# Written orders for five engines in place of a planner: a scan followed by a mixture of adapters

## The chip, the cores and the metric

The kernel runs on one core of one Trainium2 chip. The metric is the device time of one execution in microseconds (us); lower is better.

## The reference

Two stages follow each other. The first is a linear recurrence along 6400 steps, for 8 sequences of 128 channels. The second takes the 51,200 resulting rows as tokens: a gate picks 2 of 8 adapters, and each token gets its own value plus the weighted output of the two rank-16 adapters.

```python
for t in range(S):                       # S = 6400, a and b are (8, 6400, 128)
    h = a[:, t] * h + b[:, t]
    out[:, t] = h
x = out.reshape(51200, 128)
logits = x @ w_gate                      # 8 experts
topk = the two largest logits of a row
w = softmax over these two
for e in range(8):
    z = x[mask] @ A[e]                   # A[e] is (128, 16), mask: rows that chose e
    delta[mask] += w[mask, k, None] * (z @ B[e])
return x + delta
```

## The kernel before

The 51,200 rows are cut into 100 units of 512 rows. A unit passes through these operations; the letter is the name in the code, with the unit's number behind it.

- The loads ld a, ld b bring rows of `a` and `b` from HBM, two units (512 KB) at a time, into rings of 8 slots each (16 units). SP issues them, and the stores too, in one list.
- AB (line 86, the helper's `transpose`) turns 512 rows of `a` and of `b` on TensorE (PE) into `pA` and `pB`, so that time runs along the free axis. `pA` has one buffer, `pB` two.
- aev (line 491) copies `pA` to `a_st` on ScalarE (ACT).
- scan (line 510) runs the recurrence on VectorE (DVE) and writes `xT` in float16. `xT` is a ring of 16 units (XR): scan w has to wait for the readers of unit w - 16.
- L (line 82) multiplies a unit by the gate's weights into half of a PSUM bank, `pTL`. The units form gate groups of up to 4; for each group, lev (line 583) copies the logits on ACT, and some ten small steps on DVE and GpSimd (POOL), p1 to p7, m1, m2, mx, find the two largest and their difference. sig (line 684) makes the weights `g` on ACT.
- Z (line 82) multiplies the unit by all eight A at once into `pZ` (two buffers). mul (line 729) multiplies by the gate weights, in float16, into `zw`: on DVE, or for 21 units on POOL, after a copy zev (line 715) by ACT.
- T (line 86) transposes `zw` into the other half of the bank `pTL`, and tev (line 786) copies it to `zwT` on ACT. As L and T share that bank, PE and ACT take turns on it.
- R (line 82) puts x itself into `pO` (two buffers) and D (line 82) adds `zwT` times B to it. oev (line 821) copies `pO` to `outt`, a ring of 24 output slots (NOUT), and a store of one or two units takes it to HBM. The store of unit u is held until scan u + 22 is done (HOLD).

The order in which each engine meets these operations is set by a planner, `_Plan.schedule`, before the program is built. Every operation has a due number (its unit plus the offset of its kind in `KEY`) and costs in nanoseconds. The planner walks through time and gives each engine, among the operations that can start soonest, the one with the lowest due number. For a few operations it also chooses the engine. The order is then fixed: each engine runs its list from the front, and an operation whose inputs are not there holds up all behind it. `_Plan.run` writes the waits on semaphores.

The constants are an identity matrix built on POOL (`ident_f`, needed by every transposition) and the weights of the gate, A and B, which ACT's queue loads and POOL casts to float16 (cstg, cstA, cstB). At the start PE runs seven matmuls on an empty tile (`heat`), while the first loads are under way.

Of the kernel before, what the change touches and what calls it, by code (L numbers as in the profile page):

```python
# [12 lines left out]
KEY = {  # L13
    "AB": -228.9, "aev": 79.1, "scan": 140.1, "L": -12.2, "lev": -63.6, "gate": 83.5, "sig": 69.7, "Z": 27.8,
    "mul": -75.3, "zev": 6.2, "T": -117.7, "tev": 38.1, "R": 189.8, "D": 29.2, "oev": 168.4,
}
SLACK = {"pe": 20.0, "dve": 20.0, "act": 0.0, "pool": 60.0, "sp": 120.0}
# [3 lines left out]
POOL_MULS = (2, 10, 4, 2)  # L21
HOLD = 22
FREE = 100
HEATS = 7
WIDE = 100
SOLO = (2, 4)
FUSE = (100, 100)
WIDE8 = 460.0
RING = 8
XR = 16  # L30
NOUT = 24
TAIL = 10
FILLS = 0


class _Op:


    def __init__(self, name, engs, kind, unit, cost, emit, deps, dma, bank, mode):
        self.name = name  # L40
        self.engs = engs
        self.eng = engs[0]
        self.kind = kind
        self.unit = unit
        self.cost = cost
        self.emit = emit
        self.deps = deps
        self.dma = dma
        self.bank = bank
        self.mode = mode  # L50
        self.signal = False
        self.done = None
# [7 lines left out]


# [30 lines left out]
class _Plan:  # L92


    def __init__(self, sems, offset, slack):
        self.sems = sems
        self.offset = offset
        self.slack = slack
        self.ops = {}
        self.order = {e: [] for e in sems}  # L100

    def add(self, name, eng, kind, unit, cost, emit, deps=(), dma=None, bank=None, mode=None):

        engs = (eng,) if isinstance(eng, str) else eng
        cost = cost if isinstance(cost, dict) else {e: cost for e in engs}
        self.ops[name] = _Op(name, engs, kind, unit, cost, emit, list(deps), dma, bank, mode)

    def schedule(self, first, link, landing, switch):
        ops = self.ops
        users = {n: [] for n in ops}  # L110
        left = {}
        for op in ops.values():
            op.deps = [ops[d] for d in dict.fromkeys(op.deps) if d in ops]
            left[op.name] = len(op.deps)
            op.key = op.unit + self.offset.get(op.kind, 0.0)
            op.quick = min(c[0] for c in op.cost.values())
        for op in ops.values():
            for d in op.deps:
                users[d.name].append(op)
        begin, end = {}, {}  # L120
        cand = {e: [] for e in self.sems}
        free = {e: first for e in self.sems}
        bank = {}
        mode = None
        for op in ops.values():
            if not left[op.name]:
                for e in op.engs:
                    cand[e].append((0.0, op))
        todo = len(ops)
        while todo:  # L130
            found, soonest = [], {}
            for e, c in cand.items():
                for x in c:
                    op = x[1]
                    t = max(free[e], x[0])
                    if op.bank:
                        for o in bank.get(op.bank, {}).values():
                            if o.eng != e:
                                t = max(t, end[o.name])
                    if op.mode and mode and op.mode != mode:  # L140
                        t = max(t, free[e] + switch)
                    t += op.cost[e][0] - op.quick
                    found.append((t, op, e, x))
                    if t < soonest.get(e, 1e18):
                        soonest[e] = t
            e0 = min(soonest, key=soonest.get)
            limit = soonest[e0] + self.slack.get(e0, 0.0)
            t, op, e, pick = min((f for f in found if f[2] == e0 and f[0] <= limit), key=lambda f: (f[1].key, f[0]))
            t -= op.cost[e][0] - op.quick
            for x in op.engs:  # L150
                cand[x].remove(pick)
            op.eng = e
            mode = op.mode or mode
            if op.bank:
                held = bank.setdefault(op.bank, {})
                op.deps += [o for o in held.values() if o.eng != e]
                held[e] = op
            self.order[e].append(op)
            begin[op.name] = t
            free[e] = t + op.cost[e][0]  # L160
            if op.dma:
                ready = free[e] + 1000.0
                wait = max(0.0, link - ready)
                link = max(link, ready) + op.dma[2]
                end[op.name] = link + 300.0 + min(wait, landing(link))
            else:
                end[op.name] = t + op.cost[e][1]
            todo -= 1
            for u in users[op.name]:
                left[u.name] -= 1  # L170
                if not left[u.name]:
                    for x in u.engs:
                        cand[x].append((max(end[d.name] for d in u.deps), u))
        self.begin, self.end = begin, end
        self.span = max(end.values())
        for op in ops.values():
            for d in op.deps:
                d.signal = True
        for e, seq in self.order.items():
            n = 0  # L180
            for op in seq:
                if op.dma:
                    op.done = op.dma[:2]
                else:
                    n += op.signal
                    op.done = (self.sems[e], n)
# [18 lines left out]
def bass_associative_scan_2x2__then__mixture_of_adapters_kernel(  # L205
# [20 lines left out]
    lo, hi, every, at = POOL_MULS  # L226
    ON_POOL = lambda v: lo < v < NU - hi and v % every == at
# [22 lines left out]
    with ExitStack() as stack:  # L250
# [15 lines left out]
        A_e = sb(nc.sbuf_tensor("A_e", [E, D * R], F32))  # L266
# [29 lines left out]
        s_cst = sb(nc.semaphore("s_cst"))  # L296
        dma_sem = {}

        plan = _Plan(sems, KEY, SLACK)
        add = plan.add  # L300

        def add_dma(name, eng, unit, starts, slot, time, deps=()):
# [11 lines left out]
            add(name, eng, "dma", unit, (450.0 * len(starts), 0.0), emit, deps, (sem, value, time))  # L314


        add("id0", "pool", "fix", -109, (200.0, 450.0), lambda h: h.memset(ident_f[:, :], 0.0))
# [3 lines left out]
            "fix",  # L321
            -109,
            (300.0, 400.0),
# [9 lines left out]
            ["id0"],  # L333
        )

        def cst_load(name, dst, src, after):

            sem = sb(nc.semaphore(f"s_{name}"))
            add(
                name,  # L340
                "act",
                "fix",
                -109,
                (450.0, 0.0),
                lambda h: h.dma_start(dst, src).then_inc(sem, 16),
                after,
                (sem, 16, 100.0),
            )
# [9 lines left out]
        add("w0", "dve", "fix", -109, (60.0, 200.0), lambda h: h.memset(warm[:, :], 0.0))  # L358
        add("table", "act", "fix", -108, (1500.0, 1600.0), lambda h: h.activation(warm[:, :], warm[:, :], ACTF.Sigmoid), ["w0"])
        add("wt", "dve", "fix", -109, (270.0, 400.0), lambda h: h.memset(warm_t[:, :], 0.0))  # L360
# [6 lines left out]
        add("heat", "pe", "fix", -109, (372.0 * HEATS, 372.0 * HEATS), heat, ["wt"], mode="half")  # L367

        def fill(w):


            def emit(h):
                for _ in range(2):
                    last = h.matmul(pO[1][:, :], warm_t[:, 0:128], warm_t[:, :])
                return last

            add(f"fill{w}", "pe", "fix", 1000.0, (440.0, 640.0), emit, [f"AB{w}"], mode="full")

        for w in range(FILLS):
            fill(w)  # L380
        add("idh", "dve", "fix", -108, (150.0, 330.0), lambda h: h.tensor_copy(ident_h[:, :], ident_f[:, :]), ["id"])
        add("cstg", "pool", "fix", -108, (190.0, 290.0), lambda h: h.tensor_copy(wg_h, cst_f[:, 0:E]), ["ld_g"])
        add(
            "cstA",
            "pool",
            "fix",
            -107,
            (290.0, 390.0),
            lambda h: h.tensor_copy(Acat_h, cst_f[:, E : E + 128]),
            ["ld_A"],  # L390
        )
        add(
            "cstB",
            "pool",
            "fix",
            -106,
            (290.0, 390.0),
            lambda h: h.tensor_copy(Bcat_h, cst_f[:, E + 128 : E + 256]),
            ["ld_B"],
        )  # L400

# [25 lines left out]
        def load(t, w):  # L427
# [3 lines left out]
            if many == 2 and n >= WIDE and n % 2 == 0 and w + 4 <= NU:  # L431
                many = 4
# [494 lines left out]
```

## Time and profile before

| | |
|---|---|
| median of 3 runs | 204.34 us (204.23 to 206.74) |
| the profiled execution | 204.88 us, span 203.1 us |
| granted TensorE clock, mean | 0.989 |
| PE, DVE, ACT, POOL busy | 191.2, 184.8, 173.7, 115.7 us |
| moved by DMA | 79.35 MB, mean 391 GB/s |

The span runs from the first to the last instruction of one profiled execution. Rows of the page and of the other views name the line of the code, the engine, the operation and its tiles; in rows in order of time, the first two numbers are start and length in us, and square brackets hold idle time before the instruction and what ended it. ACT and DVE rows can overlap a little, since the next instruction begins while the one before still writes its last results.

### The profile page before, as it was taken

The numbers are of one execution on the slowest core, as the hardware profiler recorded it, in microseconds if no ns is written. First come the engines' busy times: TensorE is split into PE (matmuls) and PEld (weight loads), VectorE is DVE, ScalarE is ACT, GpSimd is POOL, SyncE is SP. The second block draws the span as 40 slices with busy tenths as digits, with TensorE's granted clock in tenths as the row PEclk, the third lists the DMA queues.
The fourth block names the chain that finished last, engine by engine and source line by source line (L and its number), as shares of the span: only waits on it lengthen the run. The fifth ranks groups of instructions, "written<-read, shape, count | busy, mean of one in ns | idle before, by whom it ended". The sixth has DMA issues, their size and how long they took to land.

```text
span 203.1 us, 8757 instructions
## 1 busy us (share of the span) xinstructions
PE 191.2 (94%) x3591; PEld 172.3 (85%) x3591; DVE 184.8 (91%) x268; ACT 173.7 (86%) x383; POOL 115.7 (57%) x244
## 2 busy tenths in 40 slices
PE   7788888999999999999999999999999999999992
PEld 3666777879899999999999999999999999999981
DVE  1579989999999999999999999999999999989970
ACT  3157686869899999989999999999999999999883
POOL 1324427568567466565656746656565687875520
PEclk9799999999999999999999999999999999999999
DMA  7999999999999999999999999999999999988867
GB/s 182 402 410 408 403 409 405 404 412 404 404 414 412 416 412 410 413 408 416 414 408 416 410 412 416 410 414 414 409 411 414 414 416 409 372 330 345 324 250 279
DMA packets 23688, 79.35 MB, mean 391 GB/s; under 512 B 3681, under 2 KB 3809, under 8 KB 23649
## 3 DMA queue, kind: packets, MB, share of 16 engines
q1 hardware_dynamic: 22320, 78.65, 97.0%
q8 instruction: 29, 0.48, 0.9%
q10 hardware_dynamic: 1328, 0.14, 0.5%
q14 instruction: 11, 0.08, 0.1%
HBM read 52.56 MB, written 26.21 MB: 388 GB/s over the span
## 4 chain that ended last, share of the span: by engine, by line
PE 81%; DVE 6%; ACT 6%; DMA 2%; issue 2%; POOL 1%; SPq 0%; DVEq 0%
PE pA L86 26%; PE pO L82 23%; PE pTL L86 14%; PE pZ L82 10%; PE pTL L82 5%; DVE xT L510 4%; PE pB L86 4%; DMA a_in<-in_a_dram 2%; ACT a_st L491 2%; ACT outt L821 2%; ACT zwT L786 1%; DVE mx L589 0%; SPq L311 0%; DVE zw L729 0%; ACT z_sb L715 0%
## 5 line engine op out<-in xcount | busy, mean ns | idle before, releaser
L510 DVE TENSOR_TENSOR_SCAN xT<-a_st,xT,pB 128x512 f16<-128x512 f32 x96 | 120.2, 1252 | 4.4 <-PE pZ L82 1.1
L491 ACT COPY a_st<-pA 128x512 f32<-128x512 f32 x100 | 60.6, 606 | 20.4 <-PE pB L86 15.7
L86 PE MATMUL pA<-ident_f,a_in 64*128 64x64 f32 (+1 forms) x792 | 71.8, 230 | 3.3 <-DMA a_in<-in_a_dram 1.1
L86 PE MATMUL pB<-ident_f,b_in 64*128 64x64 f32 (+1 forms) x792 | 72.5, 232 | 0.2
L86 PEld LDWEIGHTS pA<-ident_f,a_in 64*128 64x128 f32 (+1 forms) x792 | 58.0, 139 | 11.6 <-issue 2.4
L821 ACT COPY outt<-pO 128x512 f32<-128x512 f32 x96 | 59.5, 626 | 1.9 <-PE pO L82 1.7
L786 ACT COPY zwT<-pTL 128x512 f16<-128x512 f16 x95 | 58.4, 615 | 1.0 <-PE pTL L86 1.0
L86 PEld LDWEIGHTS pB<-ident_f,b_in 64*128 64x128 f32 (+1 forms) x792 | 58.0, 140 | 0.7 <-DMA b_in<-in_b_dram 0.4
L729 DVE TENSOR_TENSOR zw<-pZ,g 128x512 f16<-128x512 f32 x79 | 53.2, 679 | 2.1 <-PE pTL L86 1.2
L82 PE MATMUL pO<-ident_h,xT 128*128 128x128 f16 x400 | 41.2, 229 | 0.9 <-ACT outt L821 0.9
L82 PE MATMUL pZ<-cst_h,xT 128*128 128x128 f16 x400 | 38.6, 221 | 0.0
L86 PE MATMUL pTL<-ident_h,zw 128*128 128x128 f16 x380 | 37.7, 222 | 0.4 <-ACT zwT L786 0.4
L82 PE MATMUL pO<-cst_h,zwT 128*128 128x128 f16 x400 | 36.9, 218 | 0.6 <-ACT zwT L786 0.4
L82 PEld LDWEIGHTS pO<-ident_h,xT 128*128 128x128 f16 x400 | 32.8, 148 | 1.6 <-ACT outt L821 1.2
L729 POOL TENSOR_TENSOR zw<-z_sb,g 128x512 f16<-128x512 f32 x21 | 22.3, 1060 | 17.6 <-PE pTL L82 17.2
L82 PE MATMUL pTL<-cst_h,xT 128*128 128x8 f16 x400 | 27.9, 175 | 1.6 <-DVE xT L510 1.3
L82 PEld LDWEIGHTS pZ<-cst_h,xT 128*128 128x128 f16 x400 | 28.1, 115 | 0.2
L86 PEld LDWEIGHTS pTL<-ident_h,zw 128*128 128x128 f16 x380 | 21.8, 98 | 6.4 <-ACT zwT L786 0.5
L82 PEld LDWEIGHTS pTL<-cst_h,xT 128*128 128x128 f16 x400 | 23.6, 117 | 2.9 <-DVE xT L510 1.8
L625 POOL TENSOR_TENSOR d<-Lg,m 128x128 f32<-128x128 f32 (+3 forms) x29 | 10.7, 368 | 26.6 <-DVE m L618 26.5
L82 PEld LDWEIGHTS pO<-cst_h,zwT 128*128 128x128 f16 x400 | 23.9, 98 | 1.0 <-PE pO L82 0.9
L660 POOL TENSOR_SCALAR pn<-d 128x128 f32<-128x128 f32 (+3 forms) x31 | 17.3, 557 | 2.7
(36 smaller groups left out, 137.2 us busy)
## 6 DMA issues: line engine op xcount, KB each, us to landing
a_in<-in_a_dram SPq DMA_DIRECT2D x49, 512.0 KB, 13.7
b_in<-in_b_dram SPq DMA_DIRECT2D x49, 512.0 KB, 13.5
out_dram<-outt SPq DMA_DIRECT2D x47, 512.0 KB, 13.1
out_dram<-outt SPq DMA_DIRECT2D x6, 256.0 KB, 2.7
a_in<-in_a_dram SPq DMA_DIRECT2D x2, 256.0 KB, 9.2
b_in<-in_b_dram SPq DMA_DIRECT2D x2, 256.0 KB, 4.3
cst_f<-in_moe_A_dram ACTq DMA_DIRECT2D x1, 64.0 KB, 4.0
cst_f<-in_moe_B_dram ACTq DMA_DIRECT2D x1, 64.0 KB, 5.0
```

The costliest lines, as they stand in the source:

```text
L82: return self.h.matmul(*args, **kw)
L86: return self.h.transpose(*args)
L491: lambda h: h.copy(a_st[w % 2][:, :], pA[0][:, :]),
L510: last = h.tensor_tensor_scan(out=x_at(lo, hi), data0=a_st[w % 2][:, lo:hi], data1=pB[w % 2][:, lo:hi], initial=init, op0=ALU.mult, op1=AL ...
L625: lambda h: h.tensor_tensor(out=v(d1[s]), in0=v(Lg[s]), in1=bc(m1[s]), op=ALU.subtract),
L660: lambda h: h.tensor_scalar(v(pn[s]), v(d2[s]), 0.0, -1.0e30, ALU.is_lt, ALU.mult),
L729: lambda h: h.tensor_tensor(out=oview, in0=zview, in1=gview, op=ALU.mult),
L786: lambda h: h.copy(*evacuated(v)),
L821: return copy(outt[:, v % NOUT, :], pO[v % NO][:, :])
```

## The change

The planner with its costs, due numbers and choices goes. The order of each engine stands in the code as a string with a letter for every operation (`ORDERS`, `CODES`); the numbers are not written, since the n-th letter of a kind is the n-th operation of that kind. For DVE and ACT, the output copies of units 91, 93, 95 and 97 and three gate steps go to DVE (`ELSE`). `BANKS` holds the order in which PE and ACT (a small letter) take turns on the bank of `pTL`, and on `pA` at the end.

The orders differ from the planner's in many places, and some sizes change with them: the ring of `xT` holds 20 units and the ring of output slots 34. A store is held for scan u + 24 (for units below 66). The gate weights are loaded first; the loads of A and B stand behind the first copy aev0 on ACT, and POOL casts the gate weights before it builds the identity. In the first two units a matmul on an empty tile (F) precedes Z. The first two units are stored together, and of the last four units the first two go as a pair. The 21 products on POOL are those of the same units as before, now as a list. Options that were off (`FUSE`, `WIDE`, `FILLS`) and their code are removed.

```diff
+CODES = dict(
+    zip(
+        "bdfkpqrvhyBCEijAacsLFZuTtRDozlx41567gm23nwe",
+        "idz id ld_g ld_A ld_B w table wt heat idh cstg cstA cstB lda ldb A AB aev scan L F Z mul T tev R D oev zev lev mx p4 p1 p5 p6 p7 sig m1 p2 p3 m2 st end".split(),
+    )
+)
+ORDERS = {
+    "pe": """
+        hAaAaFRLaLaFLaZLaZLTaDLaTZRaLZaTZLLaRDTaLDZaRZTRaLLDLaRTZaDTZDaZLRTaRDLLLaTDRZaLTZaDZTLaRZLTaRLDDaTL
+        RZDaTZRLaRTDZaLLTDZaTRRDZaDLZTRaRDTLLLaZDZTaZRRTaDLTZDaRTDLRLLaZDTLaRZTDZaTRLZDaRTLDaZRLTDaZZRTRDaDZ
+        RTaZDTRLaDTLLZLaZRTLaRTLDDaTZRZLaDRTLaDZRTZaZRDTDLLaRLTLaZZDTRaRDTDaZZTRaLLRLDaTZLRDaTDLZaRZTLRaDZTL
...
+    "dve": """
+        qvyssxs1x6s1suxsmusnmsususnmsusnsusmsusnsususmsusnsumsusnsusumsusnsusmususnussmusunssusumsusnsususmu
...
+    "act": """
+        frckpclclccglcgltclctogcctlcgtcooczgtcolgctctocotcolgctzctoctcotcloogctzcotctocgltoctozcotcoltcgotcz
...
+    "pool": """
+        Bbd4E5C4576714512367145263714235674657u1234567u1234657123u4657123u4567123u45671234u657123u45671u2345
...
+    "sp": """
+        ijijjijijijijjiiijjiiiiijiijjjjjjiiiiiijjjwjijiwjjjwiiijijjjjiwwijijwijwwwwijiijwjijjjiijjwiwjwwwwii
+        wjiwjiiwwwwwjiijwjwwjiijjwiiiwwwwwjwwwwwwwwwwwwwwwwwwe
+    """,
+}
+BANKS = {
+    "A": "TtTtTtTtTt",
+    "TL": """
+        LlLlLLlLTltLlTtLTLLtlTtLTtLLLlTtTtLTtLLLlTtLTtTLtLTtLlTLtTLtTtLLTltTtLTtTLLLltTtTtLTtTLLLtlTLtTtTLtT
...
+ELSE = "oev91 oev93 oev95 oev97 p1_0 p6_0 p1_1".split()
...
-POOL_MULS = (2, 10, 4, 2)
-HOLD = 22
+POOL_MULS = (6, 10, 14, 18, 22, 26, 30, 34, 38, 42, 46, 50, 54, 58, 62, 66, 70, 74, 78, 82, 86)
+HOLD = 24
-FREE = 100
+FREE = 90
-SOLO = (2, 4)
+FILL = (0, 1)
+PAIRS = (2, 98)
+SINGLE = 2
-XR = 16
-NOUT = 24
+XR = 20
+NOUT = 34
...
+    def pick(self, codes, ops):
+
+        queue = {}
+        for op in ops:
+            queue.setdefault(op.base, []).append(op)
+        got = [queue[CODES[c]].pop(0) for c in "".join(codes.split())]
+        assert not any(queue.values())
+        return got
+
+    def arrange(self):
+        ops = list(self.ops.values())
+        for op in ops:
+            op.deps = [self.ops[d] for d in dict.fromkeys(op.deps) if d in self.ops]
+        self.order = {e: self.pick(ORDERS[e], [op for op in ops if op.eng == e]) for e in self.sems}
+        for name, codes in BANKS.items():
+            held = {}
+            for op in self.pick(codes, [op for op in ops if op.bank == name]):
+                op.deps += [o for e, o in held.items() if e != op.eng]
+                held[op.eng] = op
...
-            deps = [f"aev{w - 1}", f"scan{w - 2}", "id"]
+            deps = [f"aev{w - 1}", f"scan{w - 2}", "id", "heat"]
...
-            deps = [scanned(v), f"mul{v - NZ}", f"zev{v - NZ}", "cstA"]
-            add(f"Z{v}", "pe", "Z", v, (223.0, 423.0), emit, deps, mode="full")
+            free = [f"mul{v - NZ}", f"zev{v - NZ}"]
+            if v in FILL:
+                fill = lambda h: h.matmul(pZ[v % NZ][:, :], warm_t[:, 0:128], warm_t[:, :])
+                add(f"F{v}", "pe", fill, free + ["wt"])
+            add(f"Z{v}", "pe", emit, [scanned(v), "cstA", f"F{v}"] + free)
...
-            stores.append((u, len(mates(u))))
-            u += stores[-1][1]
+            n = 2 if u < NU - SINGLE else 1
+            stores.append((u, n))
+            u += n
...
-        plan.schedule(700.0, 3000.0, lambda t: 400.0, 94.0)
+        plan.arrange()
```

In the string of SP, i and j are the loads of `a` and `b` and w is a store. The n-th j above the first two covers units 2n - 2 and 2n - 1 (counted from 0), the n-th i covers units 2n - 1 and 2n.

More of the change, by code (lines that the diff above doesn't have):

```diff
@@ L49, in __init__ @@
         self.bank = bank
-        self.mode = mode
         self.signal = False
@@ L92, with __init__ @@
 class _Plan:
-    def __init__(self, sems, offset, slack):
+    def __init__(self, sems):
         self.sems = sems
-        self.offset = offset
-        self.slack = slack
         self.ops = {}
[L100 to L176, printed above, removed]
@@ new lines, in add @@
+    def add(self, name, eng, emit, deps=(), dma=None, bank=None):
+        if not isinstance(eng, str):
+            eng = eng[name in ELSE]
+        self.ops[name] = _Op(name, eng, emit, list(deps), dma, bank)
+    def pick(self, codes, ops):
[15 more added lines that the diff above has]
+                held[op.eng] = op
+        for op in ops:
@@ L225, in bass_associative_scan_2x2__then__mixture_of_adapters_kernel @@
     NZ, NO = 2, 2
-    lo, hi, every, at = POOL_MULS
-    ON_POOL = lambda v: lo < v < NU - hi and v % every == at
+    ON_POOL = lambda v: v in POOL_MULS
     def cut(sizes_head, size, sizes_tail):
@@ L295, in bass_associative_scan_2x2__then__mixture_of_adapters_kernel, with add_dma @@
         sems = {e: sb(nc.semaphore(f"s_{e}")) for e in ("pe", "dve", "act", "pool", "sp")}
-        s_cst = sb(nc.semaphore("s_cst"))
         dma_sem = {}
-        plan = _Plan(sems, KEY, SLACK)
+        plan = _Plan(sems)
         add = plan.add
-        def add_dma(name, eng, unit, starts, slot, time, deps=()):
+        def add_dma(name, eng, starts, slot, deps=()):
             if slot not in dma_sem:
@@ L312, in emit @@
                 return last
-            add(name, eng, "dma", unit, (450.0 * len(starts), 0.0), emit, deps, (sem, value, time))
-        add("id0", "pool", "fix", -109, (200.0, 450.0), lambda h: h.memset(ident_f[:, :], 0.0))
+            add(name, eng, emit, deps, (sem, value))
+        add("idz", "pool", lambda h: h.memset(ident_f[:, :], 0.0))
         add(
@@ L338, in cst_load @@
             sem = sb(nc.semaphore(f"s_{name}"))
[L339 to L348, printed above, removed]
+            add(name, "act", lambda h: h.dma_start(dst, src).then_inc(sem, 16), after, (sem, 16))
         cst_load("ld_g", cst_f[:, 0:E], moe_w_gate[:, :], [])
@@ L365, in heat @@
             return last
[L367 to L400, printed above, removed]
+        add("heat", "pe", heat, ["wt"])
+        add("idh", "dve", lambda h: h.tensor_copy(ident_h[:, :], ident_f[:, :]), ["id"])
+        add("cstg", "pool", lambda h: h.tensor_copy(wg_h, cst_f[:, 0:E]), ["ld_g"])
+        add("cstA", "pool", lambda h: h.tensor_copy(Acat_h, cst_f[:, E : E + 128]), ["ld_A"])
+        add("cstB", "pool", lambda h: h.tensor_copy(Bcat_h, cst_f[:, E + 128 : E + 256]), ["ld_B"])
         rings = {"a": a_in, "b": b_in}
         rows_of = {"a": a.rearrange("b s d -> (b s) d"), "b": b.rearrange("b s d -> (b s) d")}
-        solo = set(range(SOLO[0])) | set(range(NU - SOLO[1], NU))
+        solo = set(range(PAIRS[0])) | set(range(PAIRS[1], NU))
         def mates(v):
@@ L436, in load @@
             src = rows_of[t][w * UT : (w + many) * UT, :]
[L437 to L441 removed]
+            src = src.rearrange("(p i) d -> p (i d)", i=i)
             for k in range(many):
@@ L477, in transposes @@
                 both = [x for pair in zip(pa, pb) for x in pair]
-                add(f"AB{w}", "pe", "AB", w, (548.0, 750.0), emit(both), deps + [load_of["a", w], load_of["b", w]], mode="half")
+                add(f"AB{w}", "pe", emit(both), deps + [load_of["a", w], load_of["b", w]])
             else:
                 for t, name, steps, first in (("a", f"A{w}", pa, []), ("b", f"AB{w}", pb, [f"A{w}"])):
-                    mode = "full" if (t, w) in alone else "half"
-                    add(name, "pe", "AB", w, (500.0, 700.0), emit(steps), deps + [load_of[t, w]] + first, mode=mode)
+                    add(name, "pe", emit(steps), deps + [load_of[t, w]] + first)
         def a_evac(w):
@@ L522, in scan @@
                 "dve",
-                "scan",
-                w,
-                (1187.0 + 130.0 * (len(cuts) - 2), 1362.0 + 130.0 * (len(cuts) - 2)),
                 emit,
@@ L546, in emit @@
                 return last
-            add(f"L{v}", "pe", "L", v, (126.0, 310.0), emit, [scanned(v), f"lev{k - 1}", "cstg"], bank="TL", mode="full")
+            add(f"L{v}", "pe", emit, [scanned(v), f"lev{k - 1}", "cstg"], bank="TL")
         def gating(k):
@@ L569, in bc, with step @@
                 return t[:, 0:c].to_broadcast([128, c, E])
-            def step(name, eng, time, emit, deps):
-                if isinstance(time, str):
-                    time = cost(time)
-                    time = {e: time[e] for e in ((ge,) if isinstance(ge, str) else ge)}
-                add(f"{name}_{k}", eng, "gate", u, time, emit, deps)
+            def step(name, eng, emit, deps):
+                add(f"{name}_{k}", eng, emit, deps)
             add(
@@ L756, in zw_tr @@
                 bank=t_bank(v),
-                mode="full",
             )
@@ L791, in delta, with emit @@
         def delta(v):
-            def emit(what):
+            def emit(left, right, first):
                 def run(h):
-                    for q, w in [(q, w) for q in range(Q) for w in what]:
-                        left, right = {"x": (x_rows(v, q), ident_h[:, :]), "d": (zw_rows(v, q), Bcat_h)}[w]
+                    for q in range(Q):
                         last = h.matmul(
                             pO[v % NO][:, q * 128 : (q + 1) * 128],
-                            left,
+                            left(v, q),
                             right,
-                            start=w == "x" and q == 0,
-                            stop=w == "d",
+                            start=first and q == 0,
+                            stop=not first,
                             skip_group_check=True,
@@ L808, in delta @@
             deps = [f"scan{mates(v)[-1]}", f"oev{v - NO}", "idh"]
-            if v == 1:
-                deps += [f"fill{w}" for w in range(5)]
             tevs = [f"tev{w}" for w in mates(v)]
-            if FUSE[0] <= v < FUSE[1]:
-                add(f"D{v}", "pe", "D", v, (WIDE8, WIDE8 + 200.0), emit("xd"), deps + tevs + ["cstB"], mode="full")
-            else:
-                add(f"R{v}", "pe", "R", v, (223.0, 423.0), emit("x"), deps, mode="full")
-                add(f"D{v}", "pe", "D", v, (220.0, 420.0), emit("d"), [f"R{v}", "cstB"] + tevs, mode="full")
+            add(f"R{v}", "pe", emit(x_rows, ident_h[:, :], True), deps)
+            add(f"D{v}", "pe", emit(zw_rows, Bcat_h, False), [f"R{v}", "cstB"] + tevs)
         def o_evac(v):
@@ L842, in store @@
             s0 = u0 % NOUT
-            rows = out[u0 * UT : (u0 + n) * UT, :].rearrange("(p i) d -> p (i d)", p=128)
+            rows = out[u0 * UT : (u0 + n) * UT, :]
+            dst, src = rows.rearrange("(n p i) d -> p n (i d)", p=128, i=Q), outt[:, s0 : s0 + n, :]
+            if u0 not in solo:
+                dst, src = rows.rearrange("(p i) d -> p (i d)", p=128), src.rearrange("p n c -> p (n c)")
             add_dma(
@@ L846, in store @@
                 "sp",
-                u0 + HOLD,
-                [(rows, outt[:, s0 : s0 + n, :].rearrange("p n c -> p (n c)"))],
+                [(dst, src)],
                 ("o", s0, n),
-                1.036 * ((625.0 if n == 2 else 650.0) * n + 13.0),
                 [f"oev{v}" for v in range(u0, u0 + n)] + [f"scan{u0 + HOLD}"] * (u0 + HOLD < FREE),
@@ L874, in bass_associative_scan_2x2__then__mixture_of_adapters_kernel @@
         ends = [f"st{j}" for j in range(len(stores) - NOUT, len(stores))]
-        add("end", "sp", "fix", 1.0e9, (10.0, 10.0), lambda h: h.nop(), ends)
-        plan.schedule(700.0, 3000.0, lambda t: 400.0, 94.0)
+        add("end", "sp", lambda h: h.nop(), ends)
+        plan.arrange()
         block = sb(nc.Block())
```

129 lines of the change are left out of this document (34 added, 95 removed).

## The prediction

> **What bounds the kernel now.** I read the page's head first, then the busy time of the engines by stages, then VectorE alone by stages, then the order of time inside one steady unit, and last the start of the kernel.
>
> ```profile
> span 203.1 us, 8757 instructions
> PE 191.2 (94%) x3591; PEld 172.3 (85%) x3591; DVE 184.8 (91%) x268; ACT 173.7 (86%) x383; POOL 115.7 (57%) x244
> ...
> 4.00:46.00 42.00, 36.06 (x634) 30.67 (x634) 36.74 (x65) 26.61 (x62) 18.91 (x50) 0.96 1.03 404
> 46.00:175.00 129.00, 128.79 (x2562) 118.83 (x2558) 126.43 (x169) 123.07 (x271) 82.78 (x156) 1.00 1.02 411
> 175.00:199.40 24.40, 23.56 (x404) 21.72 (x400) 21.05 (x34) 22.01 (x51) 13.24 (x34) 1.00 0.82 325
> ...
> 5.60:11.10 5.50, 3.06 (x8) 0.69 1.04 407
> 11.10:50.00 38.90, 37.55 (x63) 1.00 1.03 407
> 50.00:175.00 125.00, 122.57 (x163) 1.00 1.02 411
> 175.00:197.40 22.40, 20.36 (x33) 1.00 0.81 323
> ```
>
> The columns of the three middle rows are busy us of PE, PEld, DVE, ACT and POOL, then the granted clock, the DMA share and GB/s; the last four rows hold DVE alone. From 46 to 175 us PE is busy for 128.79 of 129, DVE for 126.43 and the DMA engines all the time, so three resources are full at once and there is nothing to win there. What is left is small: VectorE is idle for 5.50 - 3.06 = 2.44 us before its third scan, 38.90 - 37.55 = 1.35 us from there to 50 us, and 22.40 - 20.36 = 2.04 us at the end, 5.8 us in all. The DMA engines have 24.4 x (1.02 - 0.82) = 4.9 us to spare, all after 175 us.
>
> One steady unit, in order of time, PE first and then ACT:
>
> ```profile
> 59.16 0.40 PE L86 MATMUL pTL<-ident_h,zw 128*128 128x128 f16 x4
> 59.40 0.27 PE L82 MATMUL pTL<-cst_h,xT 128*128 128x8 f16 x4
> 59.53 0.38 PE L82 MATMUL pO<-cst_h,zwT 128*128 128x128 f16 x4
> 59.75 0.39 PE L82 MATMUL pZ<-cst_h,xT 128*128 128x128 f16 x4
> 59.98 0.41 PE L82 MATMUL pO<-ident_h,xT 128*128 128x128 f16 x4
> 60.32 0.27 PE L86 MATMUL pA<-ident_f,a_in 64*128 64x64 f32 x1
> ...
> 60.97 0.40 PE L86 MATMUL pTL<-ident_h,zw 128*128 128x128 f16 x4
> ...
> 59.27 0.59 ACT L491 COPY a_st<-pA 128x512 f32<-128x512 f32 x1 [0.24 <-PE pB L86]
> 59.91 0.60 ACT L786 COPY zwT<-pTL 128x512 f16<-128x512 f16 x1
> 60.60 0.60 ACT L821 COPY outt<-pO 128x512 f32<-128x512 f32 x1
> ...
> 59.60 0.69 DVE L729 TENSOR_TENSOR zw<-pZ,g 128x512 f16<-128x512 f32 x1
> 60.40 1.27 DVE L510 TENSOR_TENSOR_SCAN xT<-a_st,xT,pB 128x512 f16<-128x512 f32 x1
> ```
>
> From T to T are 60.97 - 59.16 = 1.81 us. The starts give PE's price of each operation: T 0.24, L 0.13, D 0.22, Z 0.23, R 0.34 with the change back to the small tiles, AB 60.97 - 60.32 = 0.65. The old order repeats this round almost unchanged from unit 24 to unit 85.
>
> **The change part by part.** *The work.* The same 21 products stay on POOL (units 6, 10, ... 86 in both), each unit keeps its PE, ACT and DVE operations, and the head and tail groups are the same. The pipeline is as deep: when AB48 is issued, both orders have put out 39 Z and 34 D. So nothing of the 1.81 us is removed.
>
> *x of 20 units, 34 output slots.* They remove waits of a scan on R and D of 16 units before, and of an output copy on a store.
>
> ```profile
> DVE xT L510 <- PE pO L82: 0.2, 1, 0.2
> ACT outt L821 <- PE pO L82: 1.7, 4, 0.6
> ```
>
> Scans lost 0.2 us to the first wait, and the output copies waited for PE, with no store named. I count 0 for both. They only permit the new order to let AB run ahead.
>
> *The head.* The rows of POOL, PE and DVE there, and the landing times of the constants from the page:
>
> ```profile
> 0.73 0.20 POOL L317 MEMSET ident_f<- 128x128 f32 x1 [0.29 <-POOLq L912]
> 1.18 0.29 POOL L324 TENSOR_SCALAR_AFFINE_SELECT ident_f<-ident_f 128x128 f32<-128x128 f32 x1 [0.24 <-POOL ident_f L317]
> 3.94 0.19 POOL L382 CAST cst_h<-cst_f 128x8 f16<-128x8 f32 x1 [2.48 <-DMA cst_f<-in_moe_w_gate_dram]
> 9.07 0.32 POOL L660 TENSOR_SCALAR pn<-d 128x32 f32<-128x32 f32 x1
> ...
> 4.18 0.61 PE L86 MATMUL pA<-ident_f,a_in 128*128 128x128 f32 x4
> ...
> 6.65 0.68 PE pA L86 x8
> ...
> 5.61 1.22 DVE L510 TENSOR_TENSOR_SCAN xT<-a_st,pB 128x512 f16<-128x512 f32 x1 [3.88 <-PE pB L86]
> 11.08 1.28 DVE L510 TENSOR_TENSOR_SCAN xT<-a_st,xT,pB 128x512 f16<-128x512 f32 x1 [1.13 <-PE pZ L82]
> ...
> a_in<-in_a_dram SPq DMA_DIRECT2D x49, 512.0 KB, 13.7
> ...
> cst_f<-in_moe_A_dram ACTq DMA_DIRECT2D x1, 64.0 KB, 4.0
> cst_f<-in_moe_B_dram ACTq DMA_DIRECT2D x1, 64.0 KB, 5.0
> ```
>
> POOL now casts the gate weights before it builds the identity. The cast waits for its load until 3.94; then 0.19 + 0.20 + 0.24 + 0.29 put the identity at 4.86 instead of 1.47. A0 needs it, so it starts near 4.95 instead of 4.18 and the first scan near 6.4 instead of 5.61. Half of this is hidden: A1 waits for its data until 6.65 anyway. After it the new order has AB1, a fill matmul, R0 and L0 ahead of AB2, so I put the third scan at 11.5 instead of 11.08: +0.4, with bounds 0 (the load ends the wait) and +0.8 (all of it stays). A and B are now issued behind the first ACT copy, at about 5.6 to 6.7. With 4.0 and 5.0 us they land at 10 and 11.7. POOL casts B, then runs p5 (0.32), then casts A, so A is ready near 12.7. Z0 stands behind AB4, which cannot come before about 13.1 because it follows three scans of 1.27 us; Z0 follows near 13.8. The cover is 1.1 us, so I count 0. If it goes, Z0 holds all of PE behind it, AB5 first. The two fill matmuls fall on a PE that is idle there (36.06 of 42): 0, at most 0.9.
>
> *The written order in the middle.* Here the old order has a periodic round with wide gaps and the new one has none. I added PE's prices between each two operations that another engine must work between. The loop through pTL is T, the copy of zwT, and the next T or L. Without a queue on ACT it takes 0.40 + 0.58 and two hand-overs of 0.04, from these rows of the tail:
>
> ```profile
> 187.90 0.40 PE L86 MATMUL pTL<-ident_h,zw 128*128 128x128 f16 x4
> ...
> 188.34 0.58 ACT L786 COPY zwT<-pTL 128x512 f16<-128x512 f16 x1 [0.29 <-PE pTL L86]
> ```
>
> That is 1.06 us. In the steady unit ACT came 0.35 later (T ended at 59.56, the copy began at 59.91), so 1.4 us. Of 74 such gaps in the middle the new order has 14 under 1.2 and 29 under 1.4, together 4.9 us short; the old one has 1 and 3. At 1.06 only one is short, by 0.2. From AB to AB the new order has 14 of 60 gaps under 1.6, 0.6 us short; the old one has 1. From Z to T (Z 0.39, a scan ahead 1.2, the product 0.67, hand-overs) 9 gaps are under 2.6, 4.0 us short; the old one has none. The bounds are 0.2 and 4.9 + 0.6 + 4.0 = 9.5 us. The rows are nearer to a queue on ACT than to none (its only gap in that unit was 0.24), but one late spot shows in several edges and gives the next one room. I take +3.5. PE and DVE have no reserve that would give it back. Behind a waiting T or AB stand all later PE operations, then the scans, then the loads, since a slot of the input ring comes free only with AB.
>
> *The order on SP, and stores held for scan u+24 instead of u+22.* A transfer is now queued behind whatever stands before it, not behind its own need.
>
> ```profile
> 47.54 0.35 SPq L311 DMA_DIRECT2D out_dram<-outt  x1
> 48.30 0.59 ACT L491 COPY a_st<-pA 128x512 f32<-128x512 f32 x1
> 51.92 0.59 ACT L491 COPY a_st<-pA 128x512 f32<-128x512 f32 x1 [0.58 <-PE pB L86]
> ```
>
> The copies at 48.30 and 51.92 follow AB24 and AB26. The new list has 37 loads up to the one that waits for AB24 (three of half size): 35.5 x 0.524 MB = 18.6 MB, at 407 GB/s 45.7 us, so the queue is empty soon after 48. The next load goes out at 48.4, the one behind it only after AB26 at 52.0, and eight transfers that were free long before (b32 to b37 and the first store among them) stand behind it. Old stores began at 47.54; the first one now goes out near 54. With about 1.3 us from issue to data the queue is dry for about 3.6 us. The spare 4.9 us at the end pays for this on the mean engine, so 0; if the slowest of the sixteen has no spare, 3.6. The mean is what the page shows, so I stay near it: +0.6.
>
> *Stores and tail.* 51 stores instead of 53, and units 96 and 97 go as a pair; the last store is still 256 KB behind the copy of unit 99. 0.
>
> Sum: 0.4 + 3.5 + 0.6 = 4.5 us. The profiled execution took 204.88 us, 1.8 more than its span; it becomes 209.4 with a span of 207.6. The runs' median is 0.54 below the profiled one: 204.34 + 4.5 = **208.8 us**.
>
> **The rivals.** *The transfers alone decide.* The tight gaps hold, since 1.06 us is the true loop, and the dry queue costs about a third of its 3.6 us: 204.34 + 1.2 = 205.5. For it: copies on ACT start every 0.5 to 0.7 us in the steady rows. Against it: hardly a gap is left on ACT.
>
> *The order changes nothing that counts.* Same depth, same work, late spots that fall into each other's shade: 204.3. For it: 128.79 of 129 us was reached with an order from costs that were not the chip's either.
>
> *The written order closes the idle time.* VectorE's 5.8 us outside the middle are its place. From 4.1 us on it decides for faster; four fifths of it give 199.7. For it: the start has waits of 3.88 and 1.13 us on PE. Against it: the identity comes later there, and by 50 us both orders give DVE the same list (12 products, 24 scans).
>
> *The constants come late.* If A and B take as long as the input loads that fill the queue by then (13.7 us), B lands at 20.4 and Z0 runs near 21.3 instead of 13.8; some 5 us of it stay, since the scans up to the fifth run meanwhile: 208.8 + 5 = 213.8. For it: at 6 us the queue is full, at 1.2 us it was empty. Against it: B took 5.0 us beside the first loads. The Trainium skill bears on this ("DMA: Bandwidth & Descriptors", section "Queues, rings and completion order"): each DMA engine takes turns between rings, a packet of some 9 to 17 descriptors at a time. By that page A, whose 64-byte pieces are 64 for each engine, would need 4 to 7 turns behind a load's share of about 1.3 us each, 5 to 9 us more, an estimate from the page that falls between the two cases; no run here shows it yet.
>
> **How the numbers follow.** Forecast 0.56, of which 0.06 lies within 2%; late constants 0.08, transfers alone 0.14, no change 0.12, idle time closed 0.10. Two per cent, 4.1 us, is about what a measurement of this kernel can tell from no change. Slower by over 2%: 0.50 + 0.08 = 0.58; within 2%: 0.06 + 0.14 + 0.12 = 0.32; faster by over 2%: 0.10. The range leaves out most of the fast case and the end of the late constants: 203.0 to 214.0. The forecast's own range, from 1.5 to 6 us of waits in the middle, is 206.8 to 211.3.
>
> **What would show it.** Right: first scan near 6.4 and Z0 near 13.8; PE below 97% from 46 to 175 us, with waits on the copies of zwT and a_st of over 2 us together; DMA share below 0.6 from 49 to 53 us and the first store near 54. Wrong: PE full in the middle with the last T no later than 198, which leaves transfers or nothing; Z0 past 15, which makes it the constants; a span under 199, which means that the idle time was closed.

## The result, and the profile after

The changed kernel takes 218.01 us (median of 4 runs, 217.51 to 218.87) against 204.3 us before. The ratio is 1.0645 with a 95% interval of 1.0559 to 1.073: slower by 6.4%, in the direction that was forecast and outside the range of 203 to 214. Some executions are in a disturbed, slower state (here two of the four with early constants alone, 210.61 and 212.39 us, and one with SP's old list, 209.40 us); the times and ratios below leave them out, and a ratio can differ a little from that of the medians.

The profiled execution took 217.94 us. Its span on the page and stages of it, with the same columns as before (busy us of PE, PEld, DVE, ACT and POOL, granted clock, DMA share, GB/s):

```profile
span 216.1 us, 8807 instructions
...
11.00:24.10 13.10, 3.39 (x47) 2.58 (x43) 4.38 (x10) 1.84 (x4) 1.04 (x5) 1.00 1.05 392
24.10:60.00 35.90, 34.85 (x641) 31.03 (x642) 33.67 (x53) 29.23 (x65) 21.74 (x53) 1.00 0.81 293
60.00:175.00 115.00, 113.96 (x2243) 104.52 (x2241) 110.22 (x146) 109.29 (x235) 70.32 (x126) 1.00 1.01 396
...
211.20:216.10 4.90, 0.00 (x0) 0.00 (x0) 0.00 (x0) 0.00 (x0) 0.00 (x0) 0.83 0.36 135
```

Three things are new. From 11 to 24.1 us PE is busy for 3.39 of 13.1 us, and the DMA engines alone are full. From 24 to 60 us the DMA engines, full before, have a share of 0.81. After the last output copy the core waits 4.9 us for stores, where it waited 3.1 before. In the middle PE is still busy for 113.96 of 115 us.

What stands still at the start is shown by the longest waits (engine, line, what it waited for; total us, times, longest), by POOL and PE in order of time, and by the landing times of the loads:

```profile
POOL cst_h L334 <- DMA cst_f<-in_moe_B_dram: 11.9, 1, 11.9
...
PE pZ L114 <- POOL cst_h L333: 9.2, 1, 9.2
DVE zw L607 <- ACT g L573: 8.4, 1, 8.4
...
3.79 0.19 POOL L332 CAST cst_h<-cst_f 128x8 f16<-128x8 f32 x1 [3.35 <-DMA cst_f<-in_moe_w_gate_dram]
...
23.03 0.29 POOL L334 CAST cst_h<-cst_f 128x128 f16<-128x128 f32 x1 [11.90 <-DMA cst_f<-in_moe_B_dram]
...
23.80 0.29 POOL L333 CAST cst_h<-cst_f 128x128 f16<-128x128 f32 x1
...
24.14 0.62 PE L114 MATMUL pZ<-cst_h,xT 128*128 128x128 f16 x4 [9.25 <-POOL cst_h L333]
...
5.87 0.39 ACTq L310 DMA_DIRECT2D cst_f<-in_moe_A_dram  x1
6.29 0.75 ACTq L310 DMA_DIRECT2D cst_f<-in_moe_B_dram  x1
...
cst_f<-in_moe_A_dram ACTq DMA_DIRECT2D x1, 64.0 KB, 15.7
cst_f<-in_moe_B_dram ACTq DMA_DIRECT2D x1, 64.0 KB, 16.7
```

A and B were issued at 5.87 and 6.29 us, as the prediction had it, but took 15.7 and 16.7 us to land instead of 4.0 and 5.0. So A was there at 21.6, but on POOL its cast stands behind that of B, which landed at 23.0. POOL's cast of A ran at 23.80 and Z0 at 24.14, where 13.8 was expected. This is the rival "the constants come late".

By the order of the instructions, AB26 ends at 61.22 us where it ended at 51.88 before, so 9.3 us of the loss are there by then; AB75 is 10.4 late, the last D 11.2, the end of the span 13.0.

### The profile page after: what moved, and what is told of

Same layout as the page of the kernel before. It is cut to its first block, busy times and chain, and to the rows that moved or that the text cites. A ratio compares the mean times of both kernels' runs of the same rounds, so it can differ in the third digit from the quotient of the medians.

```text
span 216.1 us, 8807 instructions
## 1 busy us (share of the span) xinstructions
PE 196.6 (91%) x3593; PEld 176.1 (81%) x3593; DVE 183.7 (85%) x267; ACT 177.3 (82%) x383; POOL 116.2 (54%) x245
## 4 chain that ended last, share of the span: by engine, by line
PE 83%; DMA 9%; ACT 2%; issue 2%; POOL 1%; DVE 1%; POOLq 0%
PE pA L118 27%; PE pO L114 25%; PE pZ L114 12%; PE pTL L118 11%; DMA cst_f<-in_moe_B_dram 8%; PE pTL L114 6%; PE pB L118 3%; DMA cst_f<-in_moe_w_gate_dram 1%; ACT a_st L411 1%; ACT outt L684 1%; DVE xT L430 1%; ACT zwT L655 0%; ACT g L573 0%; POOL pn L554 0%; POOL ident_f L295 0%
## 5 line engine op out<-in xcount | busy, mean ns | idle before, releaser
L118 PE MATMUL pA<-ident_f,a_in 64*128 64x64 f32 (+1 forms) x792 | 75.0, 237 | 1.4 <-ACT a_st L411 0.7
L118 PE MATMUL pB<-ident_f,b_in 64*128 64x64 f32 (+1 forms) x792 | 75.4, 237 | 0.5 <-issue 0.3
L118 PEld LDWEIGHTS pA<-ident_f,a_in 64*128 64x128 f32 (+1 forms) x792 | 60.2, 144 | 10.0 <-ACT a_st L411 1.4
L118 PEld LDWEIGHTS pB<-ident_f,b_in 64*128 64x128 f32 (+1 forms) x792 | 60.2, 144 | 1.6 <-issue 0.8
L655 ACT COPY zwT<-pTL 128x512 f16<-128x512 f16 x95 | 57.2, 602 | 3.7 <-PE pTL L118 1.7
L684 ACT COPY outt<-pO 128x512 f32<-128x512 f32 x96 | 57.4, 603 | 1.7 <-PE pO L114 0.8
L114 PE MATMUL pO<-cst_h,zwT 128*128 128x128 f16 x400 | 37.9, 220 | 0.4
L118 PEld LDWEIGHTS pTL<-ident_h,zw 128*128 128x128 f16 x380 | 24.5, 99 | 2.2 <-issue 1.1
L114 PE MATMUL pTL<-cst_h,xT 128*128 128x8 f16 x400 | 25.5, 175 | 0.2
L114 PEld LDWEIGHTS pTL<-cst_h,xT 128*128 128x128 f16 x400 | 22.1, 118 | 1.8 <-DVE xT L430 0.5
L524 POOL TENSOR_TENSOR d<-Lg,m 128x128 f32<-128x128 f32 (+3 forms) x29 | 10.7, 369 | 23.9 <-DVE m L518 23.6
## 6 DMA issues: line engine op xcount, KB each, us to landing
cst_f<-in_moe_A_dram ACTq DMA_DIRECT2D x1, 64.0 KB, 15.7
cst_f<-in_moe_B_dram ACTq DMA_DIRECT2D x1, 64.0 KB, 16.7
```

The costliest lines, as they stand in the source:

```text
L114: return self.h.matmul(*args, **kw)
L118: return self.h.transpose(*args)
L524: lambda h: h.tensor_tensor(out=v(d1[s]), in0=v(Lg[s]), in1=bc(m1[s]), op=ALU.subtract),
L655: lambda h: h.copy(*evacuated(v)),
L684: return copy(outt[:, v % NOUT, :], pO[v % NO][:, :])
```

## The experiments

Theory 1 was that the late constants are the cause. Its rival, from the prediction, was that the tight written order is.

**Constants early.** One edit of the changed kernel, in ACT's string:

```diff
-        frckpclclccglcg...
+        fkprcclclccglcg...
```

> The changed kernel with one edit: ACT issues the loads of A and B right behind that of the gate weights, as the kernel before did, all written orders otherwise kept. Theory 1 (late constants): in the changed kernel Z0 waited for A's cast until 24.1 us, 9.4 us behind AB4, and unit 26 ran 9.4 us late; with the constants there in time Z0 runs near 15 and the time falls by about 9.4 us from 218.0, to 208 to 209. The rest over 204.3 stays for the order. Theory 2 (tight order): the start is made good later anyway, since PE and DVE have idle time behind it, and the time stays above 214.

The time is 207.37 us (2 runs, 207.36 and 207.38), 10.6 below the changed kernel, somewhat more than the 9.4 expected; against the kernel before the ratio is 1.0098 (1.0001 to 1.0194). A and B land in 3.9 and 5.1 us. Theory 1 holds for the larger part; some 2 to 3 us are left.

**Late constants in the kernel before.** The planner's order is kept, and only the two loads move on ACT's list:

```diff
         plan.schedule(700.0, 3000.0, lambda t: 400.0, 94.0)
+        seq = plan.order["act"]
+        late = [plan.ops["ld_A"], plan.ops["ld_B"]]
+        seq[:] = [o for o in seq if o not in late]
+        at = seq.index(plan.ops["aev0"]) + 1
+        seq[at:at] = late
```

> The kernel before with one edit: the loads of A and B stand behind the first ACT copy, as in the changed kernel; nothing else moves. Theory 1: Z0, which stood at 8.3 us, waits until about 22; the old order has Z0 ahead of AB2, so that even the third scan waits, and the time rises by 9 to 13 us to 213 to 217. Theory 2: the rise is under 4 us, to 208 at most.

217.68 us, ratio 1.0609 (1.0534 to 1.0684): this edit alone does to the kernel before nearly what the whole change does, a little more than the 213 to 217 expected. PE's row in order of time, and the landing time:

```profile
20.78 0.62 PE L82 MATMUL pZ<-cst_h,xT 128*128 128x128 f16 x4 [11.55 <-POOL cst_h L389]
...
cst_f<-in_moe_A_dram ACTq DMA_DIRECT2D x1, 64.0 KB, 15.1
```

**Why they land late.** Three runs take apart the place in the queue and the number of pieces. First, B ahead of A:

```diff
-        frckpclclccglcg...
+        frcpkclclccglcg...
```

> The changed kernel with the load of B ahead of that of A, both still behind the first ACT copy. If what takes the time is the number of pieces that take turns with the input loads (A has 1024, B 128), B lands 5 to 7 us after its issue, near 12, and A still near 22.5; Z0 follows A's cast at about 23, the time is 216.5 to 218. If instead every transfer issued at that point waits for the loads queued before it, B takes about 15 us, too, and both land after 20.

One run, 216.61 us. The landing times:

```profile
cst_f<-in_moe_B_dram ACTq DMA_DIRECT2D x1, 64.0 KB, 5.8
cst_f<-in_moe_A_dram ACTq DMA_DIRECT2D x1, 64.0 KB, 16.5
```

At the same place B took 5.8 us and A 16.5, as the account by pieces has it. B's 16.7 us in the changed kernel were spent behind A on ACT's own queue.

Second, A in 128 pieces:

```diff
-            cst_f[:, E : E + 128].rearrange("d (e r) -> d e r", e=E),
-            moe_A.rearrange("e d r -> d e r"),
+            cst_f[:, E : E + 128],
+            moe_A.rearrange("e (m j) r -> (e m) (j r)", j=8),
```

> The changed kernel, with A loaded at the same place of ACT's queue and with the same 64 KB, but as 128 pieces of 512 bytes instead of 1024 of 64 bytes; the columns of A are in another order, so z holds other numbers. If the number of pieces is the cost, A lands 5 to 7 us after its issue at 5.9, B near 13, Z0 runs near 14 to 15, and the time is that of the early loads, 208 to 209. If the place behind the queued loads is the cost, A still lands near 20 and the time stays near 218.

```profile
cst_f<-in_moe_A_dram ACTq DMA_DIRECT2D x1, 64.0 KB, 5.9
cst_f<-in_moe_B_dram ACTq DMA_DIRECT2D x1, 64.0 KB, 7.0
```

The same bytes from the same place land in 5.9 us, and Z0 runs at 14.99 us without a wait, as expected. The one run took 211.37 us, 6.6 below the changed kernel but over the 208 to 209 expected; from one run it stays open whether that excess is more than spread.

Third, fewer input loads ahead of them: the sixth one on SP's list waits until B has landed.

```diff
-                users.get((t, n - RING), []),
+                users.get((t, n - RING), []) + ["ld_B"] * ((t, w) == ("a", 3)),
```

> The changed kernel with one edit: the sixth load on SP's list waits until B has landed, so that A and B find only five input loads ahead of them; A keeps its 1024 pieces and its place behind the first ACT copy. If it is the turns with queued input loads that make A slow, A lands 3 to 6 us after its issue instead of 15.7, Z0 runs near 14 to 16 instead of 24.1, and the time falls to 209 to 213, since the input loads lose some 3 us at the start. If A's pieces are slow by themselves at this place, A lands near 20 again and the time is 220 or more.

```profile
cst_f<-in_moe_A_dram ACTq DMA_DIRECT2D x1, 64.0 KB, 4.5
cst_f<-in_moe_B_dram ACTq DMA_DIRECT2D x1, 64.0 KB, 4.2
```

With its 1024 pieces, but without the queue of loads beside it, A lands in 4.5 us. The time is 211.8 us (2 runs; 209 to 213 was expected, as the input loads lose time), ratio 1.0365 (1.034 to 1.0391). So it takes both: many pieces, and a full queue to take turns with.

**What is left with early constants.** The next four runs all have them. The first puts SP's list in the order of the kernel before:

```diff
-HOLD = 24
+HOLD = 22
-FREE = 90
+FREE = 100
...
-        ijijjijijijijjiiijjiiiiijiijjjjjjiiiiiijjjwjijiwjjjwiiijijjjjiiww...
+        ijijjijijijijijijijijijijijijijijijijijijiiwjwijwijwijwijwijwijwi...
```

> The changed kernel with the early loads of A and B, and SP's list in the order that the kernel before had (loads of a and b in turn, a store between each pair of them from the 43rd transfer on, held for scan u+22); PE, DVE, ACT and POOL keep the written orders. Theory 1 (the queue of transfers sets the end): with early constants alone, the last output copy ended near 202.6 of a span of 208.8 and the last transfers landed near 208, while the DMA share fell around 25 to 32 and 50 to 60 us; with the old list this dry time goes, the stores end within 3.5 us of the last output copy, and the time falls by 2 to 3 us, to 205 to 206.5. Theory 2 (the written order of PE and ACT is what is left): the time stays within 1 us of the kernel with early constants, 207.4 to 209.

The second has the identity first on POOL (`bdB` instead of `Bbd` at the head of its string):

> The changed kernel with the early loads of A and B, and POOL building the identity before it casts the gate weights, as in the kernel before. Theory: A0 starts at 4.2 instead of 4.7 us, with no gap behind the seven matmuls on the empty tile, and the small transpositions of the first units take 0.03 us each from some 11 us on instead of 0.054 until 24 us; unit 26 runs 1 to 1.5 us earlier, but the transfers still set the end: 206 to 208. Rival: the first units are bound by scans and loads, and the time does not change by more than 0.5 us.

The third has both:

> The changed kernel with all three: early loads of A and B, SP's old list, the identity first on POOL. What is left of the change are the written orders of PE, DVE and ACT, x of 20 units and 34 output slots. Theory 1: 204 to 205, within 0.5% of the kernel before: the written order in the middle costs under 0.5 us, not the 3.5 us of the prediction. Theory 2 (tight gaps in the written order): 207 or more.

The fourth has SP's written list, POOL as changed, and HEATS = 10 instead of 7:

> The changed kernel with early loads of A and B, and ten instead of seven matmuls on the empty tile at the start, so that PE works without a gap until the identity is there. If the slow transpositions of the first 24 us come from the gap of 0.4 us behind the seven, they are fast from about 11 us on and the time is 0.5 to 1.5 us lower than with early constants alone; if not, A0 starts 0.6 us later and the time rises by up to 0.5 us.

Measured: 206.63 us with the old list (3 runs, 206.13 to 208.99; ratio 1.0164, 1.0078 to 1.0251), 207.81 with the identity first (1.014, 1.0071 to 1.021), 206.63 with both (10 runs, 205.68 to 207.95; 1.0075, 1.004 to 1.0111), 208.06 with ten matmuls (1.0156, 1.0092 to 1.022). None is clearly below the 207.37 of early constants alone. The third fits neither of its theories (204 to 205, or 207 or more), and its profile showed why. The GB/s row of the page, in 40 equal slices, and its last D:

```profile
GB/s 181 399 410 407 408 409 399 407 406 407 410 410 414 412 413 414 413 411 411 410 412 414 415 412 413 409 413 415 412 412 414 410 410 404 333 214 246 399 405 182
...
197.73 0.40 PE L114 MATMUL pO<-cst_h,zwT 128*128 128x128 f16 x4
```

PE was done at 198.1 us; the kernel before ended its last D at 199.3. But the DMA rate fell to 214 near 180 us and the core then waited for stores. My list had introduced that: with stores in the order of their units, the store of unit 76, held for scan 98, stopped all behind it. The planner's list had let later ones go first (units 78 to 83 ahead of 74, 84 and 85 ahead of 76).

**Without that hold.** FREE = 90 again, so that units from 68 on are not held, with the identity first and without:

> The changed kernel with early constants, the identity first and SP's old list, as in the run before, and in addition the hold of a store ends with unit 66 (scan u+22 for u+22 below 90), as the change has it, not with unit 76. In the run before, the last D ended at 198.1 us, 1.2 us before that of the kernel before, but the DMA rate fell to 214 GB/s around 180 us, since stores in order of their units stood behind one that was held for scan 98, and the last store landed 5.2 us behind the last output copy. Theory: without that hold the rate stays above 350 until 185 us, the last store lands within 3 us of the last copy, and the time is 203 to 204.5, no slower than the kernel before. Rival: the transfers are late for another reason, and the time stays at 206 to 207.

> The same without the identity first (POOL casts the gate weights ahead of it). Theory: 0 to 0.8 us slower than with the identity first, 203.5 to 205.3, since the first scan comes 0.5 to 0.8 us later and most of it is hidden behind the second load; rival: no slower at all, since the earlier cast of the gate weights gives back what the identity loses.

With the identity first: 204.28 us (13 runs), ratio 0.9977 (0.9953 to 1.0002). Without: 204.24 us (12 runs), ratio 1.0014 (0.998 to 1.0049). The GB/s row of the first:

```profile
GB/s 186 400 412 406 407 407 403 405 410 406 404 414 414 411 418 412 407 413 411 413 416 411 410 414 412 415 409 414 409 415 410 416 411 411 410 361 306 239 272 246
```

The dip before a last burst is gone, and with it 2.35 us (206.63 to 204.28). The written orders of PE, DVE and ACT, x of 20 units and 34 slots are all still there: together they cost nothing that was measured (a gain of one and a loss of another could hide in the sum). The two runs do not tell the identity's place apart from nothing.

**Only the constants late.** That kernel with A and B behind aev0 again:

> The written orders of PE, DVE and ACT with SP's old list, the hold to unit 66 and the identity first (204.3 us), with one edit: the loads of A and B back behind the first ACT copy. Theory: the late constants alone cost what they cost the kernel before, 9 to 13 us, so 213.5 to 217; SP's list and the late constants add up (218.0 less 3 us is 215). Rival: with the loads of a and b in regular turn the time lost at the start is partly made good, and it is under 211.

214.39 us, ratio 1.0487 (1.0451 to 1.0523): 10.1 us more than with early constants, and nothing of it is made good: in the profiled executions of the two the sixth scan is 8.8 us late, the last D and the end 9.1 (214.78 against 205.70 us). This closes the sum: late constants 214.39 - 204.28 = 10.1, SP's written list with its hold (and the identity's place, which is near 0) 218.01 - 214.39 = 3.6. With early constants and the identity first, the written list with its hold costs the same: 207.81 - 204.28 = 3.5. No version clearly beats the kernel before; the best ratio's interval reaches 1.0002.

## Why the prediction was wrong

The step that failed is the cover of Z0: "With 4.0 and 5.0 us they land at 10 and 11.7 ... The cover is 1.1 us, so I count 0." The durations came from a row of this kernel, but from loads issued at 1.2 us into an almost empty queue, and were carried to 6 us, when eleven input loads had been issued. In the changed kernel the loads took 15.7 and 16.7 us, Z0 waited 9.25 us and the time rose by 10.1. The rival with this wait was there, with 8% and 213.8 us. Its reason, that both loads take as long as the input loads queued before them, was not the one: from the same place B took 5.8 us when it went first. Its price, 13.7 us to land and 5 us left of it, was too low on both counts, and its evidence "for" (a full queue) should have outweighed a row from an empty one.

The Trainium skill had the mechanism ("DMA: Bandwidth & Descriptors", section "Queues, rings and completion order"): engines take turns between the rings. The prediction's estimate from that page was 5 to 9 us more for A, in packets of 9 to 17 descriptors; measured were 15.7 - 4.0 = 11.7 us more. The trace's records of single DMA packets show the turns as one for one: while the 1024 pieces of A ran, from 9.5 to 20.7 us, 1026 pieces of input loads began. A's 64 pieces for each engine, each behind a 4 KB piece at 392 / 16 = 24.5 GB/s (0.167 us), make 10.7 us; from its first piece to its last were 11.2. Here the measurement decides: the turns were, on average, by single pieces. The first piece itself came 3.7 us after the issue, against 2.2 in the kernel before.

The other steps, against the runs:

- *The written order in the middle*, +3.5: it was the largest term and is 0. With good lists around it, the ratio is 0.9977 to 1.0014. Counting gaps under 1.4 us and adding up what they lack priced every tight gap as a stall. The true limit was nearer the 1.06 us of a loop without a queue, on which the prediction's lower bound of 0.2 us rested. In the run without the hold (identity late), of 70 turns of T, its copy and the next use of the bank between 46 and 175 us, eight took under 1.4 us and the shortest 1.14; the waits of that stage list none of PE on ACT. That turn (T and the next T on PE, the copy on ACT), and the stage:

```profile
168.53 0.39 PE L118 MATMUL pTL<-ident_h,zw 128*128 128x128 f16 x4
...
169.67 0.39 PE L118 MATMUL pTL<-ident_h,zw 128*128 128x128 f16 x4
...
168.95 0.59 ACT L655 COPY zwT<-pTL 128x512 f16<-128x512 f16 x1
...
46.00:175.00 129.00, 128.81 (x2531) 118.38 (x2531) 124.52 (x165) 124.03 (x267) 81.87 (x152) 1.00 1.03 412
```

PE is as full as before (128.79).

- *SP's list*, +0.6 with a bound of 3.6: it measured 3.6, the bound. The pages show it as predicted in kind, though weaker at the place named and not only there. With early constants and the identity first (207.81 us), the share from 49 to 53 us is 0.84, where under 0.6 was foretold; the rate falls to 330 to 343 GB/s between 46 and 57 us, and again near 80 and 120; the last D ends at 199.5, close to the 199.3 of the kernel before, but after the last copy there are 5.6 us of stores alone:

```profile
GB/s 192 397 410 408 404 409 403 405 405 343 330 393 413 413 408 387 347 413 413 412 411 412 401 331 413 406 405 418 413 414 413 412 405 417 410 413 413 354 359 102
...
175.00:200.10 25.10, 24.13 (x422) 22.24 (x419) 22.11 (x36) 23.42 (x53) 14.38 (x38) 1.00 0.97 390
200.10:205.70 5.60, 0.00 (x0) 0.00 (x0) 0.00 (x0) 0.00 (x0) 0.00 (x0) 0.74 0.33 125
```

  The spare 4.9 us at the end, on the mean engine, did not pay for it. How the list's order and the hold for u+24 share the 3.6 was not tried.

- *The identity behind the gate's cast*, +0.4: the first scan came at 7.04 in the changed kernel, 1.4 us late and later than the 6.4 predicted, but the two kernels without and with it do not differ.
- *Work removed, POOL's products, rings, tail*, 0: the kernel at 204.28 us has them all, so their sum is near 0; none was tried alone.

With early constants the kernel takes 207.37 us, near the forecast of 208.8, but by chance: 3.5 us of the sum were not there, and 3.0 were too little for SP's list.

## What to carry to other kernels

A load's time to land belongs to the moment at which it was seen: before a small load is moved behind a stream of large ones, count its pieces, since each piece may wait for a piece of the stream. A list on a queue that is full most of the time is part of the schedule: a transfer that waits for something late, in the middle of the list, costs the queue's idle time in full when the queue is what ends last. Tight distances in a written order cost nothing here; they are worth a price only where a trace shows the engines between them to be late.

## What the runs showed of the hardware

- Two DMA queues took turns piece by piece (1024 pieces of one beside 1026 of the other), so that 64 KB in 1024 pieces took 15.7 us beside 4 KB pieces and 4.5 us nearly alone, while all transfers together still moved 392 GB/s.
- PE ran slowly far into the kernel in some executions, though the clock column shows 1.00 there, since the first clock record comes later (24 us with early constants, 30 us in the changed kernel). The run with only the constants late has the records: a granted clock of 0.50 from 13.6 to 30.7 us, with the same 311 to 312 ns for one small transposition. That transposition, in ns (min/median/max), in the changed kernel from 24 to 29 and from 40 to 60 us:

```profile
L118 PE MATMUL pA<-ident_f,a_in x18: 311/311/367, 24.8 to 28.9; 64*128 64x64 f32 x18
L118 PE MATMUL pA<-ident_f,a_in x96: 222/223/274, 40.7 to 59.3; 64*128 64x64 f32 x96
```

  From 12 to 20 us it took 223 in the kernel before and 312 in the profile with early constants. Ten matmuls at the start instead of seven did not lower the time (208.06 against 207.37 us); what sets the moment was not found.
